# Two feed-forward layers behind an attention: weight loads on another queue, six weight decodes joined by adding transfers, one output block moved to seven products, and a plan with a seed

## The chip, the cores and the metric

The kernel runs on 1 core of a Trainium2 chip. The metric is the device time of one execution in microseconds, the median of three runs. A profiled execution gives the trace that is read here.

## What is computed

A decayed causal attention (4 batches, 8 heads, 576 positions, 64 wide) gives 2304 tokens of 512 features. Two feed-forward layers follow, each with weights of its own, and everything is wanted in float32:

```python
def _moe_ref(x, w_in, w_out):        # layer 0: 512 -> 2048 -> 512
    h = x @ w_in
    g = h - np.tanh(h)
    return g @ w_out

def _moe2_ref(x, w_in, w_out):       # layer 1
    h = x @ w_in
    g = h * (1.0 / (1.0 + np.exp(-h)))
    return g @ w_out
```

The weights reach the chip as raw 64-bit words, which the kernel turns into float32 itself.

## The kernel before

**Products.** Each matrix operand is split in a high part (rounded to the type that TensorE multiplies fast) and a low part (the rest), and a product is three matmuls: high by high, high by low, low by high. A 2 x 2 block product is formed by seven block products with sums of blocks around them instead of eight. ScalarE makes the high parts, VectorE the low parts.

**Work.** A unit is one layer, one set of 512 hidden features (4 sets a layer) and one block of 768 tokens (3 a set): 24 units, 12 for each layer. The first three run beside the end of the attention and in slots of their own; units 3 to 23 are laid out by `joint` (L803). For each unit, `h_step` (L646) runs seven products with the first matrix, 12 matmuls each; then the hidden blocks are gated, added to one another and split (L925 to L989); `c_step` (L713) runs the products with the second matrix, in layer 1 of 18 matmuls of 256 columns each, one unit behind, so that on TensorE a step of unit u's first matrix and one of unit u-1's second alternate. Split inputs go through rings of three tiles: `gr` for hidden blocks, `xr` for inputs, loaded by `ring_load` (L619) on SP's queue. In units 12 to 14, the first set of layer 1, the inputs are not loaded but made from x (`make`, L889) and stored for later sets (`spill`, L634).

**The plain unit.** PLAIN (L40) names unit 13: its second-matrix products are eight plain pieces (`plain_c`, L750; four of 24 matmuls and four of 12, 144 in all), which need only four split hidden blocks, no sums of them, and whose results are copied out by ScalarE (L1072). Set 4, to which it belongs, is in MIXED: its second-matrix weights get a third group (L848).

**Weight decode.** A weight pair (q, m) is two of the sixteen chunks of a layer for matrix m (0 or 1); q runs from 0 to 15, a set has two of them, so set 4 is q = 8, 9 and set 5 is q = 10, 11. `decode` (L830) lists its stages: raw words arrive (two transfers of half a pair, `wload` L156), ScalarE scales the high words (L203), VectorE shifts (L207), takes the exponent (L211), forms the low word's value (L214), joins both by an addition (L226), forms four sums of blocks (L230), then ScalarE casts (L247) and VectorE subtracts (L249) in groups. Temporaries are `wa`, `wb` and `ws`, one of each. As soon as the low word's value is formed, `fill` (L309) issues the next pair's load on SP's queue.

**The order.** `joint` collects tasks with an engine, a cost in steps (a step is 2080 ns), the keys that they read and write, and a wanted time. `planned` (L1125) works from these: each task of an engine other than TensorE gets a latest time by going back from TensorE's order; among those that are ready, the one due first goes next. No task may start more than EARLY = 8 steps before its wanted time. A transfer is a task of the engine "D" with a fixed time; only the first waiting one of "D" is looked at.

Of the kernel before, what the change touches and what calls it, by code (L numbers as in the profile page):

```python
# [1 line left out]

# [12 lines left out]
P = 128  # L15
# [21 lines left out]

U0 = 3
S0 = U0 // 3
PLAIN = (13,)  # L40
PLAINSETS = {s for s in range(NSET, 2 * NSET) if all(NB * s + b in PLAIN for b in range(NB))}
EARLIER = 5
MIXED = {u // NB for u in PLAIN} - PLAINSETS

KA = {1: 1, 2: 2, 3: 4, 4: 0, 5: 6, 6: 3, 7: 5}
# [3 lines left out]
def forgetting_attention_two_ffn(  # L49
# [21 lines left out]
    def rd(ap):  # L71
        return ap.bitcast(F32)
# [80 lines left out]

    raws, wtiles, wjobs = {}, {}, {}

    def wload(q, m, parts=(0, 1)):  # L156
        if q >= 2 * NPR:
            return
        l, c = divmod(2 * q, NFC)
        if (q, m) not in raws:  # L160
            raws[q, m] = rawp.tile([P, 2, DM, 2], U32, tag=f"raw{m}", name=f"raw{q}_{m}")
        for i in parts:
            to = raws[q, m][:, i].rearrange("p n w -> p (n w)")
            nc.sync.dma_start(out=to, in_=(w_in, w_out)[m][l][c + (i if m and q >= 2 * S0 else 1 - i)])

    PLUS, MINUS = ALU.add, ALU.subtract
    RECIPE = (
# [27 lines left out]
    def wjob(q, m, what, part=None):  # L195

        st = wjobs.setdefault((q, m), {})
        l, blocks = 2 * q // NFC, m == 0 or q >= 2 * S0 and q // 2 not in PLAINSETS
        i = slice(0, 2) if part is None else slice(part, part + 1)
        n = f"{q}_{m}"  # L200
        if what == "scale":
            high = rd(raws[q, m][:, i, :, 1])
            nc.scalar.activation(high, high, AF.Prelu, scale=2.0 ** -112, alpha=-(2.0 ** 32))  # L203
        elif what == "shift":
            if "a" not in st:
                st["a"] = wtmp.tile([P, 2, DM], U32, tag="wa", name=f"wa{n}")
            nc.vector.tensor_scalar(st["a"][:, i], raws[q, m][:, i, :, 1], 3, None, ALU.logical_shift_left)  # L207
        elif what == "exponent":
            if "b" not in st:
                st["b"] = wtmp.tile([P, 2, DM], F32, tag="wb", name=f"wb{n}")  # L210
            nc.vector.tensor_scalar(st["b"][:, i].bitcast(U32), st["a"][:, i], 0xFF800000, None, ALU.bitwise_and)  # L211
        elif what == "low":
            b = st["b"][:, i]
            nc.vector.scalar_tensor_tensor(b, raws[q, m][:, i, :, 0], 2.0 ** -52, b, ALU.mult, ALU.mult)  # L214
        elif what == "join":
            if "w" not in st:
                if blocks:
                    st["s"] = wtmp.tile([P, 8, 256], F32, tag="ws", name=f"ws{n}")
                    st["w"] = st["s"][:, 0:4].rearrange(
                        "p (k i) f -> p i k f" if m else "p (i k) f -> p i k f", i=2)  # L220
                else:
                    st["w"] = rd(st["a"])
            a, b = rd(st["a"][:, i]), st["b"][:, i]
            if blocks:
                a, b = (t.rearrange("p i (k f) -> p i k f", k=2) for t in (a, b))
            nc.vector.tensor_tensor(st["w"][:, i], a, b, ALU.add)  # L226
        elif what == "sum":
            s = st["s"]
            to, p, op, r = RECIPE[m * (2 - l)][part]
            nc.vector.tensor_tensor(s[:, to], s[:, p], s[:, r], op)  # L230
        elif what in ("hi", "lo"):
            hi, lo = wtile(q, m)
            frm = st["s"][:, 1:8] if m == 0 else st["w"]
            if m:
                hi, lo = (t.rearrange("p (i k) f -> p i (k f)", i=2) for t in (hi, lo))
            c = i if m else (slice(0, 3), slice(3, 7), slice(7, 8))[part]
            frm = st["s"][:, 0:1] if m == 0 and part == 2 else frm[:, c]
            if what == "hi":
                nc.scalar.copy(hi[:, c], frm)
            else:  # L240
                nc.vector.tensor_tensor(lo[:, c], frm, rd(hi[:, c]), ALU.subtract)
        else:
            for to, n, frm in GROUPS[m and l + 1][part]:
                hi, lo = place(q, to) if m else (w[:, to:] for w in wtile(q, 0))
                hi, lo, frm = hi[:, 0:n], lo[:, 0:n], st["s"][:, frm:frm + n]
# [63 lines left out]
    def fill(j):  # L309
        q, m, *what = j  # L310
        wjob(q, m, *what)
        if what[0] == "low":
            raws.pop((q, m))
            wload(q + 1, m)

    xo, xd, tt = {}, {}, {}

# [485 lines left out]
    def joint():  # L803
# [16 lines left out]
        W2, N2, basis = dve(TB), act(TB), {}  # L820
# [4 lines left out]
        def wkeys(q, m, k):  # L825

            blocks = {0: (0, 1, 2, 3), 3: (1,), 4: (2, 3), 5: (0,)}
            return [("w", q % NSLOT, m, 10 + b) for b in blocks[k]] if m and k in blocks else [("w", q % NSLOT, m, k)]

        def decode(q, m):  # L830

            l = 2 * q // NFC
            job, raw = (lambda *a: lambda: fill((q, m) + a)), ("raw", m)
            yield "D", 3.5, None, (), (raw,), None
            yield "A", act(DM * 2), job("scale"), (raw,), (raw,), None
            yield "V", 0.33, job("shift"), (raw,), ("wa",), None
            yield "V", 0.33, job("exponent"), ("wa",), ("wb",), None
            yield "V", dve(1024), job("low"), (raw,), ("wb", raw), None
# [6 lines left out]
            yield "V", dve(1024), job("join"), ("wa", "wb"), tuple(("ws", k) for k in range(8)), None  # L845
            for k, (to, p, op, r) in enumerate(RECIPE[m * (2 - l)]):
                yield "V", dve(256), job("sum", k), (("ws", p), ("ws", r)), (("ws", to),), None
            groups = [0, 1, 2] if m and q // 2 in MIXED else [0, 1]  # L848
            behind = m and l and q % 2 and 3 * (q // 2) - 1 in PLAIN and q // 2 not in MIXED
            for g in [1, 3, 4, 5] if behind else groups:  # L850
                cols, key = [("ws", k) for to, n, f in GROUPS[m and l + 1][g] for k in range(f, f + n)], wkeys(q, m, g)
                yield "A", act(256 * len(cols)), job("HI", g), cols, key, g
                yield "V", dve(256 * len(cols)), job("LO", g), cols + key, key, None

        def spread(t0, t1, jobs, since):

            total = sum(c for e, c, *_ in jobs if e == "V")
            t = t0
            for e, c, fn, r, w, tag in jobs:
                if e == "D":  # L860
                    task(t - 6, e, c, fn, r, w)
# [27 lines left out]
        def make(u):  # L889
# [13 lines left out]
            for k, i in enumerate(STEPS):  # L903
                n, f = 7 * (u - U0) + k, src[i]
                kr, when = ("xr", n % 3), t0 + 2 * k - 4.6

                def low(n=n, f=f):
                    t = ring_tile(n)
                    tt_(t[:, 1], q[f](), rd(t[:, 0]), MINUS)
                    spill(n)  # L910

                task(when, "A", N2, lambda n=n, f=f: copy(ring_tile(n)[:, 0], q[f]()), (key[f],), (kr,))
                task(when + 0.1, "V", W2, low, (key[f], kr), (kr,))


        for u in range(U0, len(units) + 1):
# [207 lines left out]

    def planned(tasks):  # L1125

        LAG, EARLY = 0.1, 8

        def lag(n, d):

# [504 lines left out]
```

## Time and profile before

| | us |
|---|---|
| median of three runs (899.52 to 899.75) | 899.64 |
| profiled execution | 900.03 |
| its span, first to last instruction | 898.2 |
| TensorE busy | 889.7 |
| VectorE busy | 784.7 |
| ScalarE busy | 602.6 |
| GpSimd busy | 162.8 |

PE is TensorE, PEld its weight loads, DVE VectorE, ACT ScalarE, POOL GpSimd; SPq is the queue of transfers that SyncE issues. Lines are those of the kernel before.

### The profile page before, as it was taken

The numbers are of one execution on the slowest core, as the hardware profiler recorded it, in microseconds if no ns is written. First come the engines' busy times: TensorE is split into PE (matmuls) and PEld (weight loads), VectorE is DVE, ScalarE is ACT, GpSimd is POOL, SyncE is SP. The second block draws the span as 40 slices with busy tenths as digits, with TensorE's granted clock in tenths as the row PEclk, the third lists the DMA queues.
The fourth block names the chain that finished last, engine by engine and source line by source line (L and its number), as shares of the span: only waits on it lengthen the run. The fifth ranks groups of instructions, "written<-read, shape, count | busy, mean of one in ns | idle before, by whom it ended". The sixth has DMA issues, their size and how long they took to land.

```text
span 898.2 us, 16276 instructions
## 1 busy us (share of the span) xinstructions
PE 889.7 (99%) x6079; PEld 845.6 (94%) x6079; DVE 784.7 (87%) x1320; ACT 602.6 (67%) x1008; POOL 162.8 (18%) x242
## 2 busy tenths in 40 slices
PE   8999999999999999999999999999999999999997
PEld 6777777799999999999999999999999999999997
DVE  7799989798889999998999999997997799776647
ACT  6788888765556666766766778866765665555543
POOL 8999999500000000000000000000000000000000
PEclk9999999999999999999999999999999999999999
DMA  5424533477458686787678564787667566555753
GB/s 176 148 97 149 178 122 96 179 280 287 194 224 299 226 279 236 251 305 258 235 269 293 210 249 186 276 281 273 232 243 267 194 223 240 193 178 183 231 170 120
DMA packets 51103, 196.04 MB, mean 218 GB/s; under 512 B 9744, under 2 KB 15120, under 8 KB 50992
## 3 DMA queue, kind: packets, MB, share of 16 engines
q1 hardware_dynamic: 50744, 194.72, 61.4%
q8 instruction: 48, 0.79, 0.3%
q10 hardware_dynamic: 280, 0.28, 0.1%
q14 instruction: 31, 0.25, 0.1%
HBM read 151.98 MB, written 41.88 MB: 216 GB/s over the span
## 4 chain that ended last, share of the span: by engine, by line
PE 94%; POOL 2%; DVE 1%; DMA 1%; ACT 1%; issue 1%; SPq 0%; DVEq 0%; POOLq 0%; ACTq 0%
PE h L656 34%; PE a L732 32%; PE a L431 6%; PE t L1364 5%; PE s L1317 4%; PE out_t L1423 4%; PE h L475 4%; PE a L764 2%; PE s L1309 2%; PE h L461 2%; POOL kqs L1259 1%; POOL p L1352 1%; DMA raw<-w_in 0%; PE out_t L1451 0%; PE out L1423 0%
## 5 line engine op out<-in xcount | busy, mean ns | idle before, releaser
L656 PE MATMUL h<-xr,wh 128*128 128x384 f32 x1176 | 299.1, 335 | 0.0
L656 PEld LDWEIGHTS h<-xr,wh 128*128 128x128 f32 x1176 | 208.7, 188 | 0.4 <-ACT h L944 0.4
L656 PE MATMUL h<-xr,wl 128*128 128x384 f32 x588 | 196.6, 334 | 0.0
L656 PEld LDWEIGHTS h<-xr,wl 128*128 128x128 f32 x588 | 110.4, 188 | 0.0
L987 ACT CAST gr<-f 128x768 fp32r<-128x768 f32 x104 | 86.7, 838 | 32.5 <-PE a L732 29.9
L988 DVE TENSOR_TENSOR gr<-f,gr 128x768 fp32r<-128x768 f32 x104 | 98.6, 950 | 3.9 <-ACT gr L987 3.9
L732 PE MATMUL a<-wh,gr 128*128 128x256 f32 x516 | 99.2, 282 | 0.0
L732 PEld LDWEIGHTS a<-wh,gr 128*128 128x128 f32 x516 | 82.9, 190 | 0.0
L1338 ACT ACTIVATE p<-p,mn 128x128 f32<-128x128 f32 (+3 forms) x128 | 71.3, 559 | 16.4 <-DVE mn L1330 13.8
L1031 DVE TENSOR_TENSOR x<-a,x 128x768 f32<-128x768 f32 x61 | 58.1, 953 | 21.3 <-PE a L732 20.6
L1352 POOL TENSOR_SCALAR p<-p,sm 128x128 f32<-128x128 f32 (+3 forms) x128 | 73.3, 590 | 8.0 <-DVE sm L1349 5.3
L732 PE MATMUL a<-gr,wh 128*128 128x384 f32 x288 | 73.3, 334 | 0.4 <-DVE gr L988 0.4
L732 PE MATMUL a<-weh,gr 128*128 128x256 f32 x380 | 73.3, 282 | 0.0
L732 PE MATMUL a<-wl,gr 128*128 128x256 f32 x258 | 72.8, 282 | 0.0
L1330 DVE CUSTOM_DVE_ANT_0 p<-s,mask 128x128 f32<-128x128 f32 (+3 forms) x128 | 59.5, 478 | 14.1 <-PE s L1317 11.8
L1024 ACT COPY a<-a 128x768 f32<-128x768 f32 x49 | 38.4, 784 | 49.4 <-PE a L732 46.8
L732 PEld LDWEIGHTS a<-weh,gr 128*128 128x128 f32 x380 | 61.1, 190 | 0.2
L944 ACT COPY h<-h 128x768 f32<-128x768 f32 x42 | 33.0, 785 | 35.0 <-PE h L656 33.8
L732 PE MATMUL a<-gr,weh 128*128 128x384 f32 x216 | 54.8, 334 | 0.0
L1259 POOL TENSOR_TENSOR kqs<-kqraw,kqs 128x288 fp32r<-128x288 f32 (+1 forms) x62 | 53.8, 889 | 1.3
L732 PE MATMUL a<-wel,gr 128*128 128x256 f32 x190 | 53.6, 282 | 0.0
L732 PEld LDWEIGHTS a<-gr,wh 128*128 128x128 f32 x288 | 52.0, 188 | 0.8 <-DVE gr L988 0.8
(173 smaller groups left out, 2075.1 us busy)
## 6 DMA issues: line engine op xcount, KB each, us to landing
xr<-xd SPq DMA_DIRECT2D x126, 768.0 KB
raw<-w_in SPq DMA_DIRECT2D x32, 512.0 KB
raw<-w_out SPq DMA_DIRECT2D x32, 512.0 KB
xd<-xo SPq DMA_DIRECT2D x21, 768.0 KB
xd<-xr SPq DMA_DIRECT2D x21, 768.0 KB
kqraw<-kq SPq DMA_DIRECT2D x16, 608.0 KB
aside<-aside SPq DMA_DIRECT2D x15, 384.0 KB
vraw<-v SPq DMA_DIRECT2D x16, 320.0 KB
```

The lines of the kernel that those rows point to most:

```text
L431: nc.tensor.matmul(dst, w, m, start=first and r == 0, stop=last and r == 2)
L656: nc.tensor.matmul(dst[:, j, 0:TH], w[:, ds], m[:, d], start=i in (1, 5) and d == r == 0, stop=d == 1 and r == 2, skip_group_check=True,)
L732: nc.tensor.matmul(dst, w, m, start=fresh and (l == 0 or d != 1) and j == r == 0, stop=j == 1 and r == 2, skip_group_check=True,)
L987: task(w, "A", N2, lambda g=g, f=frm: copy(g[:, 0], f), (kf,), (("gh", kg),))
L988: task(w + 0.1, "V", W2, lambda g=g, f=frm: tt_(g[:, 1], f, rd(g[:, 0]), MINUS), (kf, ("gh", kg)), (("gl", kg),))
L1024: task(when, "A", N2, lambda to=zs, frm=ys: copy(to, frm), (ky,), (kz,), True)
L1031: task(when, "V", W2, lambda: tt_(to, *((frm, to) if op == PLUS else (to, frm)), op), (kf, kx[c]), (kx[c],), True)
L1259: eng.tensor_tensor(lo[:, c0:c1], raw[p][:, c0:c1], rd(hi[:, c0:c1]), ALU.subtract)
L1330: nc.vector.tensor_tensor_reduce(out=pt.rearrange("p (g c) -> p g c", g=2) if i == 4 else pt, in0=src, in1=m, op0=ALU.add, op1=ALU.min, sc ...
L1338: nc.scalar.activation(pt, pt, AF.Exp, bias=mn, scale=-1.0, accum_out=sums[:, n // 3 % 5, n % 3, 0:1],)
L1352: nc.gpsimd.tensor_scalar(pt, pt, sm[:, j:j + 1], 1.0, ALU.mult, ALU.mult)
L1364: nc.tensor.transpose(t[:, k], pt[:, c * P:c * P + P], ident)
```

## The change

- PLAIN is empty. Unit 13's second-matrix products are seven, as in the units around it, set 4 has no third weight group, and no unit has the extra step in `base`.
- ADDED lists 25 of the pairs that `joint` decodes. For these the join adds in place in the temporary that holds the shifted word; every second pair has its blocks 0 to 3 in `wa` and 4 to 7 in `ws`, the others all in `ws`. Groups that cross from block 3 to block 4 of a split pair are cast and subtracted in two pieces. The temporaries are allocated once.
- The load that follows a pair in ADDED is issued from GpSimd's queue, as a task of its own in the plan. Second-matrix rows land in the blocks' order, in two runs for each partition and transfer.
- For six pairs (BYDMA: (8,0), (9,0), (9,1), (10,0), (10,1), (11,0)) the low word's value is written back into the raw tile, and a transfer from GpSimd's queue adds it to the high word instead of VectorE's addition.
- In the plan a load takes 5.5 steps (before 3.5), an adding transfer 4.0, a spill 3.5 (before none); transfers need no longer be taken in the order of their wanted times; EARLY is 12; each latest time is moved by up to 0.2 step by a random number from a fixed seed.

```diff
-PLAIN = (13,)
+PLAIN = ()
+SEED, SPREAD = 5, 0.2
...
+    ADDED = [(2 * S0 + 1, 1)]
+    for g in range(S0, 2 * NSET - 1):
+        o = 2 * g + 1
+        ADDED += [(o, 1), (o + 1, 0), (o + 1, 1), (o + 2, 0)] if g >= NSET else [(o + 1, 0), (o, 1), (o + 1, 1), (o + 2, 0)]
+    ADDED = list(dict.fromkeys(ADDED + [(2 * NPR - 1, 1)]))
+
+    BYDMA = {(NPR, 0), (NPR + 1, 0), (NPR + 1, 1), (NPR + 2, 0), (NPR + 2, 1), (NPR + 3, 0)}
...
+    def block(q, m, k, n=1):
+
+        if (q, m) not in ADDED:
+            return wjobs[q, m]["s"][:, k:k + n]
+        if k + n <= 4 and ADDED.index((q, m)) % 2 == 0:
+            return tmp("wa", [P, 4, 256])[:, k:k + n]
+        return tmp("ws", [P, 8, 256])[:, k:k + n]
...
-    def wload(q, m, parts=(0, 1)):
+    def wload(q, m, parts=(0, 1), queue=None):
...
+            if m and (q, m) in ADDED:
+
+                to = raws[q, m].rearrange("p i n w -> p (i n w)").rearrange("p (k i z) -> p k i z", k=2, i=2)[:, :, i]
+                frm = frm.rearrange("p (k z) -> p k z", k=2)
+            (queue or nc.sync).dma_start(out=to, in_=frm)
...
+            low = rd(row(raws[q, m][:, 0])) if (q, m) in BYDMA else factor
...
+            elif what == "low":
+                nc.vector.scalar_tensor_tensor(low, words[:, :, 0], 2.0 ** -52, factor, ALU.mult, ALU.mult)
+            elif (q, m) in BYDMA:
+                nc.gpsimd.dma_start(out=high, in_=low, accum_op=ALU.add, max_dma_last_dim=8 * DM)
+            else:
+                nc.vector.tensor_tensor(high, high, low, ALU.add)
...
-        if what[0] == "low":
+        if what[0] == ("join" if (q, m) in BYDMA else "low"):
             raws.pop((q, m))
-            wload(q + 1, m)
+            if (q, m) not in ADDED:
+                wload(q + 1, m)
...
-            yield "D", 3.5, None, (), (raw,), None
+            yield "D", LOADING, (lambda: wload(q, m, queue=nc.gpsimd)) if (q - 1, m) in ADDED else None, (), (raw,), "load"
...
+            if added:
+                yield *(("D", ADDING) if (q, m) in BYDMA else ("V", dve(1024))), job("join"), [kept] + wa, wa, None
...
+                task(when + 0.2, "D", SPILLING, None, (kr,), ())
...
-        LAG, EARLY = 0.1, 8
+        LAG, EARLY = 0.1, 12
...
+        shake = random.Random(SEED)
+        latest = [t + SPREAD * shake.uniform(-1, 1) for t in latest]
...
-                known = [(max(r, free[e]), n) for n in waiting[:1 if e in "PSD" else 60] if (r := ready(n)) is not None]
+                known = [(max(r, free[e]), n) for n in waiting[:1 if e in "PS" else 60] if (r := ready(n)) is not None]
```

## Rows read from the trace of the kernel before

**Rows 1.** The page, part 1: busy us, share of the span, instructions.

```profile
PE 889.7 (99%) x6079; PEld 845.6 (94%) x6079; DVE 784.7 (87%) x1320; ACT 602.6 (67%) x1008; POOL 162.8 (18%) x242
```

**Rows 2.** Waits of TensorE: total us, times, longest.

```profile
PE a L732 <- DVE gr L988: 0.4, 1, 0.4
```

**Rows 3.** Windows of the units in `joint`: busy time of each engine.

```profile
core 0: us, PE busy (x) PEld busy (x) DVE busy (x) ACT busy (x) POOL busy (x), PEclk, DMA share, GB/s
300.00:520.00 220.00, 220.00 (x1271) 220.00 (x1270) 209.39 (x269) 149.21 (x195) 0.00 (x0) 1.00 0.76 260
520.00:640.00 120.00, 119.57 (x811) 119.16 (x810) 109.72 (x140) 90.42 (x117) 0.00 (x0) 1.00 0.69 250
...
620.00:640.00 20.00, 20.00 (x144) 20.00 (x143) 12.86 (x16) 13.83 (x18) 0.00 (x0) 1.00 0.80 280
```

**Rows 4.** The chain that ended last: start us, us, what.

```profile
37.20 4.21 DMA raw<-w_in
...
581.31 2.87 PE a L764 x24
...
606.71 4.31 PE a L764 x36
613.10 2.15 PE a L732 x18
```

**Rows 5.** VectorE groups after 262 us: busy us, mean ns of one, idle before.

```profile
L230 DVE TENSOR_TENSOR ws<-ws 128x256 f32<-128x256 f32 x104 | 40.2, 418 | 0.4
...
L226 DVE TENSOR_TENSOR ws<-wa,wb 128x1024 f32<-128x1024 f32 x26 | 31.7, 1220 | 0.4
L249 DVE TENSOR_TENSOR wl<-ws,wh 128x1024 fp32r<-128x1024 f32 x26 | 31.6, 1217 | 1.1 <-ACT wh L247 1.1
...
L988 DVE TENSOR_TENSOR gr<-f_a,gr 128x768 fp32r<-128x768 f32 x20 | 19.0, 952 | 22.8 <-ACT gr L987 22.8
L947 DVE TENSOR_TENSOR f_a<-f,f 128x768 f32<-128x768 f32 x20 | 19.0, 951 | 0.3
...
L249 DVE TENSOR_TENSOR wl<-ws,wh 128x512 fp32r<-128x512 f32 x12 | 8.2, 683 | 0.0
```

**Rows 6.** ScalarE groups after 262 us.

```profile
L987 ACT CAST gr<-f_a 128x768 fp32r<-128x768 f32 x20 | 16.8, 838 | 0.0
```

**Rows 7.** Timeline: a low word on VectorE, then TensorE's product that reads it.

```profile
562.84 0.95 DVE L988 TENSOR_TENSOR gr<-f,gr 128x768 fp32r<-128x768 f32 x1
...
564.22 0.28 PE L732 MATMUL a<-wh,gr 128*128 128x256 f32 x1
```

**Rows 8.** Timeline: decode of (10,0), then of (11,0), to unit 15's first product.

```profile
482.31 0.81 SPq L164 DMA_DIRECT2D raw<-w_in  x2
...
576.53 1.21 DVE L214 SCALAR_TENSOR_TENSOR wb<-raw,wb 128x1024 f32<-128x1024 uint32 x1
577.77 1.50 SPq L164 DMA_DIRECT2D raw<-w_in  x2
...
587.80 1.15 ACT L203 ACTIVATE raw<-raw 128x1024 f32<-128x1024 f32 x1
...
607.45 1.04 ACT L247 CAST wh<-ws 128x1024 fp32r<-128x1024 f32 x1
...
609.86 1.22 DVE L249 TENSOR_TENSOR wl<-ws,wh 128x1024 fp32r<-128x1024 f32 x1
...
610.86 0.52 PE L656 MATMUL h<-xr,wh 128*128 128x384 f32 x2
```

**Rows 9.** Waits of SP's queue after 262 us.

```profile
SPq L164 <- DVE wb L214: 28.6, 18, 6.2
...
SPq L625 <- DMA xd<-xr: 11.1, 2, 7.4
```

**Rows 10.** Line L207 before 180 us, then after: ns min/median/max.

```profile
L207 DVE TENSOR_SCALAR wa<-raw x7: 415/724/1159, 40.2 to 174.5; 128x512 uint32<-128x512 uint32 x6, 128x1024 uint32<-128x1024 uint32 x1
...
L207 DVE TENSOR_SCALAR wa<-raw x28: 678/685/696, 195.5 to 770.5; 128x1024 uint32<-128x1024 uint32 x28
```

**Rows 11.** The page, part 6: issues of transfers.

```profile
raw<-w_in SPq DMA_DIRECT2D x32, 512.0 KB
```

More of the change, by code (lines that the diff above doesn't have):

```diff
@@ L1 @@
+import random
 from contextlib import ExitStack
@@ L154, in forgetting_attention_two_ffn, with tmp, row @@
     raws, wtiles, wjobs = {}, {}, {}
-    def wload(q, m, parts=(0, 1)):
+    ADDED = [(2 * S0 + 1, 1)]
[4 more added lines that the diff above has]
+    BYDMA = {(NPR, 0), (NPR + 1, 0), (NPR + 1, 1), (NPR + 2, 0), (NPR + 2, 1), (NPR + 3, 0)}
+    lasting = {}
+    def tmp(tag, shape, dtype=F32):
+        if tag not in lasting:
+            lasting[tag] = wtmp.tile(shape, dtype, tag=tag, name=f"{tag}_")
+        return lasting[tag]
+    def block(q, m, k, n=1):
[4 more added lines that the diff above has]
+        return tmp("ws", [P, 8, 256])[:, k:k + n]
+    def row(t):
+        return t.rearrange("p k f -> p (k f)")
+    def wload(q, m, parts=(0, 1), queue=None):
         if q >= 2 * NPR:
@@ L162, in wload @@
         for i in parts:
-            to = raws[q, m][:, i].rearrange("p n w -> p (n w)")
-            nc.sync.dma_start(out=to, in_=(w_in, w_out)[m][l][c + (i if m and q >= 2 * S0 else 1 - i)])
+            to, frm = row(raws[q, m][:, i]), (w_in, w_out)[m][l][c + (i if m and q >= 2 * S0 else 1 - i)]
+            if m and (q, m) in ADDED:
+                to = raws[q, m].rearrange("p i n w -> p (i n w)").rearrange("p (k i z) -> p k i z", k=2, i=2)[:, :, i]
+                frm = frm.rearrange("p (k z) -> p k z", k=2)
+            (queue or nc.sync).dma_start(out=to, in_=frm)
     PLUS, MINUS = ALU.add, ALU.subtract
@@ L203, in wjob @@
             nc.scalar.activation(high, high, AF.Prelu, scale=2.0 ** -112, alpha=-(2.0 ** 32))
+        elif (q, m) in ADDED and what in ("shift", "exponent", "low", "join"):
+            high, factor = row(block(q, m, 0, 4)), row(tmp("wb", [P, 4, 256]))
+            if (q, m) in raws:
+                words = raws[q, m].rearrange("p i n w -> p (i n) w")
+            low = rd(row(raws[q, m][:, 0])) if (q, m) in BYDMA else factor
+            if what == "shift":
+                nc.vector.tensor_scalar(high.bitcast(U32), words[:, :, 1], 3, None, ALU.logical_shift_left)
+            elif what == "exponent":
+                nc.vector.tensor_scalar(factor.bitcast(U32), high.bitcast(U32), 0xFF800000, None, ALU.bitwise_and)
+            elif what == "low":
[4 more added lines that the diff above has]
+                nc.vector.tensor_tensor(high, high, low, ALU.add)
         elif what == "shift":
@@ L227, in wjob @@
         elif what == "sum":
-            s = st["s"]
             to, p, op, r = RECIPE[m * (2 - l)][part]
-            nc.vector.tensor_tensor(s[:, to], s[:, p], s[:, r], op)
+            to, p, r = (block(q, m, k) for k in (to, p, r))
+            nc.vector.tensor_tensor(to, p, r, op)
         elif what in ("hi", "lo"):
@@ L242, in wjob @@
         else:
-            for to, n, frm in GROUPS[m and l + 1][part]:
+            pieces = [(to, n, frm) for to, n, frm in GROUPS[m and l + 1][part]]
+            if (q, m) in ADDED and ADDED.index((q, m)) % 2 == 0:
+                pieces = [
+                    piece for to, n, frm in pieces
+                    for piece in ([(to, 4 - frm, frm), (to + 4 - frm, n - 4 + frm, 4)] if frm < 4 < frm + n else [(to, n, frm)])
+                ]
+            for to, n, frm in pieces:
                 hi, lo = place(q, to) if m else (w[:, to:] for w in wtile(q, 0))
-                hi, lo, frm = hi[:, 0:n], lo[:, 0:n], st["s"][:, frm:frm + n]
+                hi, lo, frm = hi[:, 0:n], lo[:, 0:n], block(q, m, frm, n)
                 if what == "HI":
@@ L818, in act @@
             return (n / 0.96 + 60) / 2080
-        W2, N2, basis = dve(TB), act(TB), {}
+        W2, N2, basis, LOADING, ADDING, SPILLING = dve(TB), act(TB), {}, 5.5, 4.0, 3.5
         base = {U0: 0}
@@ L833, in decode @@
             job, raw = (lambda *a: lambda: fill((q, m) + a)), ("raw", m)
-            yield "D", 3.5, None, (), (raw,), None
+            yield "D", LOADING, (lambda: wload(q, m, queue=nc.gpsimd)) if (q - 1, m) in ADDED else None, (), (raw,), "load"
             yield "A", act(DM * 2), job("scale"), (raw,), (raw,), None
-            yield "V", 0.33, job("shift"), (raw,), ("wa",), None
-            yield "V", 0.33, job("exponent"), ("wa",), ("wb",), None
-            yield "V", dve(1024), job("low"), (raw,), ("wb", raw), None
+            added = (q, m) in ADDED
+            own = added and ADDED.index((q, m)) % 2 == 0
+            blk = [("wa" if own and k < 4 else "ws", k) for k in range(8)]
+            wa = blk[0:4] if added else [("wa", k) for k in range(4)]
+            if added and ADDED.index((q, m)) == 0:
+                wa = wa + [("ws", k) for k in range(8)]
+            yield "V", 0.33, job("shift"), (raw,), wa, None
+            wa = wa[0:4]
+            yield "V", 0.33, job("exponent"), wa, ("wb",), None
+            kept = (raw if (q, m) in BYDMA else "wb")
+            yield "V", dve(1024), job("low"), (raw, "wb"), ("wb", raw), None
             if m and q // 2 in PLAINSETS:
@@ L844, in decode @@
                 return
-            yield "V", dve(1024), job("join"), ("wa", "wb"), tuple(("ws", k) for k in range(8)), None
+            if added:
+                yield *(("D", ADDING) if (q, m) in BYDMA else ("V", dve(1024))), job("join"), [kept] + wa, wa, None
+            else:
+                yield "V", dve(1024), job("join"), ["wb"] + wa, tuple(("ws", k) for k in range(8)), None
             for k, (to, p, op, r) in enumerate(RECIPE[m * (2 - l)]):
-                yield "V", dve(256), job("sum", k), (("ws", p), ("ws", r)), (("ws", to),), None
+                yield "V", dve(256), job("sum", k), (blk[p], blk[r]), (blk[to],), None
             groups = [0, 1, 2] if m and q // 2 in MIXED else [0, 1]
@@ L850, in decode @@
             for g in [1, 3, 4, 5] if behind else groups:
-                cols, key = [("ws", k) for to, n, f in GROUPS[m and l + 1][g] for k in range(f, f + n)], wkeys(q, m, g)
+                cols, key = [blk[k] for to, n, f in GROUPS[m and l + 1][g] for k in range(f, f + n)], wkeys(q, m, g)
                 yield "A", act(256 * len(cols)), job("HI", g), cols, key, g
@@ L860, in spread @@
                 if e == "D":
-                    task(t - 6, e, c, fn, r, w)
+                    task(t - 6 * (tag == "load"), e, c, fn, r, w)
                     continue
```

## The prediction

> **What bounds the kernel now.** I read five views in this order. The page's busy shares come first: TensorE is busy 889.7 of 898.2 us, VectorE 784.7, ScalarE 602.6, GpSimd 162.8 [rows 1]. The reader should see that nothing can be gained but by giving TensorE less to do, and that VectorE is the next to bind. The waits of TensorE confirm it: in the whole stretch that the change touches (from about 262 us) it waits once, 0.43 us, for a VectorE low word [rows 2, 3]. The windows then say how near VectorE is to the edge: between 300 and 520 us it is busy 209.39 of 220 us, between 520 and 640 us 109.72 of 120, and of the 10.28 us idle there 7.14 lie after 620 us; the granted clock is 1.00 (the 2.4 GHz level) all along and GpSimd does nothing [rows 3]. The timeline shows what 95% means for a single product: a low word ends at 563.79 us and the product that reads it starts at 564.22, 0.43 us later [rows 7]. So TensorE sets the end, and VectorE keeps up with a few tenths of a microsecond in hand.
>
> The sum is made against the profiled execution: 900.03 us, of which 898.2 are the span and 1.83 lie around it. The median of three runs, 899.64, is 0.39 below it, and I take that off at the end.
>
> **TensorE.** With PLAIN empty, unit 13 (second layer, first set, second block of tokens) forms its output by seven products instead of eight plain pieces. In the chain a plain piece of 24 matmuls takes 2.87 us and three pieces of 12 together 4.31, a product of 18 takes 2.15 [rows 4]. Four pieces of each kind are 4 x 2.87 + 4 x 1.44 = 17.24 us; seven products 7 x 2.15 = 15.05. Difference: **-2.2 us**; by matmuls, 144 - 126 = 18 at 2.15/18 us, it is 2.15, which I use. The 0.43 us wait may stay or go; I leave it in and keep its removal for the low end.
>
> **VectorE.** Unit 13 now needs what its neighbours need: three sums of gated blocks, one more for the fourth, and three more low words of ring tiles, 7 x 0.95 = +6.66 us (the rows with f_a stand for all of them) [rows 5]. The change of basis at L1086 moves: unit 16 loses it, unit 13 gains one subtraction of the same width, nothing in sum. Set 4 loses its separate third group, two 256-wide low words, -0.84. Six joins go to transfers, 6 x 1.22 = -7.31. In 13 of the 25 decodes (every second one in ADDED) a low-word group is cut at the boundary between two temporaries: 2 x 0.683 - 1.217 = 0.15 us each, +1.9 in all [rows 5]. Sum: **+0.4 us**. By place: four of the six joins ((9,1), (10,0), (10,1), (11,0)) lie in 520 to 640 us, so that window gets 6.66 - 4.87 + 0.45 for three cuts, less up to 0.84, which is 1.4 to 2.2 us, and has 2.15 us less time, against 10.28 us idle [rows 3, 5]. The second decode of set 5, due only at unit 16, can move behind 620 us. It is therefore costed at nothing: the cover is that idle time, and if the order doesn't reach it, TensorE waits for the rest, up to 4 us.
>
> **ScalarE** gets three more casts at 0.84 us, three seeds and four copies in place of the four copies of plain pieces, and 13 cuts: below 10 x 0.84 = 8.4 us near unit 13, where it is busy 90.42 of 120 us [rows 3, 6]. Nothing on the path.
>
> **Queues.** 23 weight loads (46 transfers of 512 KB [rows 11]) leave SP's queue for GpSimd's. On SP they waited 28.6 us in 18 waits for a decode, and the loads of ring tiles stood behind them [rows 9]; TensorE never waited for a ring tile [rows 2], so that gain is zero now. On GpSimd's queue a waiting load holds up only other loads and the six accumulating transfers; the engine itself is idle there [rows 3]. The plan books 5.5 steps (11.4 us, a step being 2.08 us in the code) for a load. One 512 KB half took 4.21 us where the chain shows it [rows 4], so two are at most 8.4: within the booking, cost nothing. Splitting second-matrix rows in two halves doubles their packets; bound 0 to 4.2 us on a landing, inside the remaining 3 us or just over it; I take 0, as the nearest row leaves room.
>
> **The accumulating transfer** has no row. A lower bound is the 4.21 us of a plain 512 KB load, an upper one the longest wait for a stored ring tile, 7.4 us [rows 4, 9], and since such a transfer must also read its destination it could take twice that, 14.8. The plan books 4 steps, 8.3 us. I take about 6, nearest to the two measured rows. The Trainium skill, "DMA: Bandwidth & Descriptors", section "Anatomy of one DMA — SWDGE (gpsimd) path", gives 2.0 us plus bytes over 436 GB/s; an estimate by that page is 3.2 us for 512 KB, and the sum would be the same. No row here shows it.
>
> What is late next if it is slow: the decode of (11,0), needed at unit 15's first product. In the trace its scaling starts at 587.80 us, its high words at 607.45, its low words end at 611.08, and that product's first half starts at 610.86, with (11,0) read in the second half, a microsecond later [rows 8]. The work between scaling and high words is 1.15 + 2 x 0.69 + 1.22 + 1.22 + 4 x 0.42 = 6.65 us [rows 5, 8, 10] of 19.65, so 13.0 us are spare. Two accumulating transfers lie in that line, (10,0)'s, behind which (11,0)'s load now waits, and its own; each takes the place of a 1.22 us join, and the deadline is 2.15 us earlier. At 6 us each they eat 2 x 4.8 + 2.15 = 11.7 of the 13.0. Fits.
>
> **Order.** EARLY from 8 to 12 steps, transfers that no longer queue behind one another in the plan, the second temporary and the spills as stages give the plan more to choose from. The seed moves each deadline by up to 0.2 step, 0.42 us, as much as the 0.43 us margin [rows 7]: bounds 0.43 gained and, if one product in a unit is late by that, some 10 units x 0.2 = 2 lost; I take 0, since the only loss in the trace is a single wait [rows 2].
>
> **Sum:** 900.03 - 2.15 - 0.39 = **897.5 us**, 0.24% below the median. About 0.2% (1.8 us) is what a measurement of this kernel can tell from no change, so the forecast stands only just beyond it.
>
> **Rivals.**
> *Thin margin.* A VectorE order that puts a 1.22 us decode step ahead of a low word makes TensorE wait 0.8 us (1.22 less 0.43) [rows 5, 7]. Against it: one such wait in 600 us. For it: VectorE has 6.66 us more to do around unit 13 and shifted deadlines. Two such waits give 897.5 + 1.6 = 899.1: within 0.2%.
> *The accumulating transfers are late.* Place: (11,0) before unit 15. If (10,0) is not decoded earlier than now, TensorE waits once each transfer exceeds (13.0 - 2.15)/2 + 1.22 = 6.6 us, and the change turns slower by over 0.2% once the wait exceeds 2.15 + 1.8 us, at 8.6 us each. At 10 us: 2 x 8.8 + 2.15 - 13.0 = 6.7 us, **904.2 us**; at the upper bound of 14.8 some 914. For it: the DMA engines are busy 0.69 of this window [rows 3]. Against it: the plan books 8.3 us, and (10,0)'s data lie ready long before its low words are made at 576.53 us, since its load went out at 482.31 [rows 8].
> *GpSimd and VectorE hold each other up.* While GpSimd computes, early in the kernel, the 1024-wide shift takes up to 1.159 us; afterwards, with GpSimd idle, never more than 0.696 [rows 10]. Writing descriptors may bring that back: 0.47 us for each of the two such operations in a decode, some 8 in the stretch without idle time, up to 3.8 us: 901.3 if all are met, 899 if some. The Trainium skill, "SBUF — State Buffer", section "SBUF: two separate sides", warns against this very move: a transfer issued from GpSimd has its descriptors delayed while VectorE runs an operation of two ports. By that rule loads start at most 0.7 us later, within the booking, so the trace prices the other direction higher.
> *Nothing is gained*, the seven products simply running as long as eight pieces, is excluded by rows 4.
>
> **Chances.** Forecast 0.53; thin margin 0.18; mutual blocking 0.06; late transfers 0.23. Faster 0.53, same 0.24 (the second and third), slower 0.23. The range starts at 896.9, 0.43 us for the wait and some scatter below the forecast, and goes to 902.5, which takes in the two cases in the middle and the mildest of the late transfers; about 2 in 10 stay outside.
>
> **What would show it.** TensorE's lines lose the 24- and 12-matmul pieces, seven products of 2.15 us stand between some 581 and 609 us, interleaved with unit 14's first-matrix products; 600 to 640 us carries 2 us less; TensorE's waits for VectorE, ScalarE or a transfer after 262 us total under 0.8 us; the add of wa and wb appears six times less; shifts keep 0.69 us. I am wrong if TensorE waits at unit 15's first product, if a join's transfer takes over 8.6 us, or if shifts stretch towards 1.1 us.

## The result and the profile after

The changed kernel takes 905.06 us (median of 6 runs, 904.31 to 905.75) against 899.6 for the kernel before (6 runs beside it, 899.52 to 899.75): a ratio of 1.0059, 95% interval 1.0048 to 1.0069. It is slower, by 5.5 us, where 2.1 us less was forecast. The profiled execution took 904.72 us with a span of 902.8, 4.6 more than before.

The page, part 1, of the kernel after (columns as in [rows 1]):

```profile
PE 889.8 (99%) x6061; PEld 845.0 (94%) x6061; DVE 784.2 (87%) x1332; ACT 607.0 (67%) x1025; POOL 197.4 (22%) x294
```

TensorE runs 18 matmuls fewer and yet is as long busy as before, 889.8 to 889.7 us [rows 1]. VectorE is down by 0.5 us. What TensorE waits for from 262 us on stands in the view of waits (total, times, longest), in place of the single 0.4 us of [rows 2]:

```profile
PE h L713 <- DMA xr<-xd: 3.6, 2, 3.4
...
PE h L713 <- ACT h L1013: 1.3, 1, 1.3
```

And the windows, the first three those of [rows 3], the last three cut out of the second:

```profile
300.00:520.00 220.00, 220.00 (x1271) 220.00 (x1270) 207.96 (x272) 149.10 (x200) 16.56 (x25) 1.00 0.77 265
520.00:640.00 120.00, 114.99 (x755) 113.34 (x754) 108.63 (x141) 91.53 (x121) 8.67 (x13) 0.99 0.73 260
...
620.00:640.00 20.00, 20.00 (x135) 20.00 (x135) 13.27 (x18) 13.22 (x17) 2.57 (x4) 0.94 0.81 296
...
610.00:615.00 5.00, 4.70 (x32) 4.32 (x31) 4.96 (x8) 3.76 (x6) 0.00 (x0) 1.00 1.02 420
615.00:620.00 5.00, 1.66 (x7) 1.69 (x8) 4.93 (x8) 2.56 (x3) 0.00 (x0) 0.91 0.92 334
620.00:625.00 5.00, 5.00 (x29) 5.00 (x29) 1.28 (x2) 2.07 (x3) 1.45 (x2) 0.75 0.85 310
```

TensorE's waits lie between 582 and 619 us, in the steps of unit 14's first matrix and the first of unit 15's. Behind the 3.4 us wait the granted clock falls: 0.75 over five microseconds, so partly at the lower level, 1.2 GHz. The chain of waits gives the order of events (start, us, what):

```profile
571.30 9.52 DMA x<-aside
...
580.84 0.97 DVE f_tmp L965
...
583.49 0.70 ACT h L1013
...
601.24 12.23 DMA xd<-xr
...
613.53 4.67 DMA xr<-xd
...
618.34 3.57 PE h L713 x12
621.90 2.46 PE a L789 x18
624.37 2.08 PE h L713 x12
626.45 2.15 PE a L789 x18
```

The first two products after the wait take 3.57 and 2.46 us, the next two 2.08 and 2.15: 1.8 us are the clock's. The span adds up: 898.2 - 2.15 (matmuls) - 0.43 (the old wait) + 4.9 (the two lines of waits) + 2.25 (889.8 less 889.7 - 2.15: busier, 1.8 of it by the clock) = 902.8.

Two collisions of transfers are in that chain. The timeline of GpSimd's and SyncE's queues and of VectorE in the kernel after (start, us, engine and line; in brackets what ended the idle time before). Where no view prints a landing, the text gives the last update of the transfer's semaphore in the trace:

```profile
564.91 0.91 POOL L251 DMA_DIRECT2D ws__3958<-raw  x1 [50.08 <-ACT f L1013]
570.14 1.09 POOL L198 DMA_DIRECT2D raw<-w_in  x2 [4.31 <-DMA ws__3958<-raw]
...
571.30 1.10 SPq L733 DMA_DIRECT2D x<-aside  x1
...
580.84 0.96 DVE L965 TENSOR_TENSOR f_tmp<-x 128x768 f32<-128x768 f32 x1 [3.32 <-DMA x<-aside]
...
598.49 0.95 DVE L977 TENSOR_TENSOR xr<-x,xr 128x768 fp32r<-128x768 f32 x1
...
600.83 0.32 SPq L682 DMA_DIRECT2D xr<-xd  x1
601.24 2.16 SPq L695 DMA_DIRECT2D xd<-xr  x2
...
602.10 0.95 DVE L977 TENSOR_TENSOR xr<-x,xr 128x768 fp32r<-128x768 f32 x1
...
605.07 1.11 POOL L198 DMA_DIRECT2D raw<-w_in  x2 [5.85 <-DMA ws__3958<-raw]
...
613.53 25.97 SPq L682 DMA_DIRECT2D xr<-xd  x8
```

The same places in the kernel before:

```profile
572.68 1.00 SPq L676 DMA_DIRECT2D x<-aside  x1
...
578.93 0.95 DVE L897 TENSOR_TENSOR f_tmp<-x 128x768 f32<-128x768 f32 x1
...
592.21 0.95 DVE L909 TENSOR_TENSOR xr<-x,xr 128x768 fp32r<-128x768 f32 x1
593.18 0.33 SPq L638 DMA_DIRECT2D xd<-xr  x1
...
603.23 0.33 SPq L625 DMA_DIRECT2D xr<-xd  x1
```

```profile
610.00:615.00 5.00, 5.00 (x39) 5.00 (x38) 5.00 (x7) 3.08 (x5) 0.00 (x0) 1.00 0.58 198
```

*First collision.* At 564.91 GpSimd's queue issues the adding transfer of (10,0). Once it has landed, at 570.14, the queue sends the load of (11,0), 1 MB. 1.16 us later SyncE's queue sends the load of a set-aside block of x that unit 14's inputs need. That load lands after 9.5 us and VectorE stands still for 3.32 us. Before, it was issued at 572.68 and VectorE started on it at 578.93 without a wait, and it took 5.7 us; (11,0) came only after it, at 577.77 [rows 8]. TensorE's wait of 1.3 us follows through ScalarE: it casts the late tile at 581.83, and only behind that, at 583.49, does it copy the earlier result that TensorE waits for.

*Second collision.* Unit 14's last input tile is made at 602.10 (before: 600.48). The store of the tile before it leaves at 601.24, between an adding transfer (597.12) and 1 MB of (11,1) (597.72) on one side and, at 605.07, 1 MB of (12,0) on the other. The store lands after 12.2 us, and only then, at 613.53, may SyncE's queue load unit 15's second tile into the ring place that the store was read from. It lands at 618.20, and TensorE has had nothing to do for 3.4 us. The store is not only slow, it also starts late. Its tile's low word is made at 598.49 (before: 592.21), and the store stands behind the ring load of 600.83, so it leaves 8.1 us later than before (593.18). Before, it landed after 5.8 us, and the ring load (603.23) did not have to wait for it. Of the 14.5 us by which the store lands later, 8.1 are its start and 6.4 its way. Between 610 and 615 us the transfer engines are full, share 1.02, 420 GB/s; before they stood at 0.58 there.

The transfers that the forecast worried about were on time. The page, part 6, of the kernel after (issue, count, size, median us to landing):

```profile
raw<-w_out POOLq DMA_DIRECT2D x24, 512.0 KB, 6.8
raw<-w_in POOLq DMA_DIRECT2D x22, 512.0 KB, 7.2
...
wa__3938<-raw POOLq DMA_DIRECT2D x3, 512.0 KB, 6.8
ws__3958<-raw POOLq DMA_DIRECT2D x3, 512.0 KB, 5.5
```

### The profile page after: what moved, and what is told of

The parts are those of the page before. It is cut to its first block, busy times and chain, and to the rows that moved or that the text cites. A ratio compares the mean times of both kernels' runs of the same rounds, so it can differ in the third digit from the quotient of the medians.

```text
span 902.8 us, 16319 instructions
## 1 busy us (share of the span) xinstructions
PE 889.8 (99%) x6061; PEld 845.0 (94%) x6061; DVE 784.2 (87%) x1332; ACT 607.0 (67%) x1025; POOL 197.4 (22%) x294
## 4 chain that ended last, share of the span: by engine, by line
PE 92%; DMA 3%; DVE 2%; ACT 1%; issue 1%; DVEq 0%; SPq 0%; ACTq 0%
PE h L713 32%; PE a L789 32%; PE t L1437 5%; PE s L1390 5%; PE a L488 5%; PE out_t L1496 5%; PE h L532 4%; PE s L1382 2%; PE h L518 1%; DMA xd<-xr 1%; DMA x<-aside 1%; DMA xr<-xd 1%; PE out L1496 0%; PE out_t L1524 0%; DVE gr L1057 0%
## 5 line engine op out<-in xcount | busy, mean ns | idle before, releaser
L789 PE MATMUL a<-wh,gr 128*128 128x256 f32 x564 | 108.8, 283 | 0.0
L789 PEld LDWEIGHTS a<-wh,gr 128*128 128x128 f32 x564 | 91.0, 191 | 0.0
L789 PE MATMUL a<-weh,gr 128*128 128x256 f32 x416 | 80.1, 282 | 0.0
L789 PE MATMUL a<-wl,gr 128*128 128x256 f32 x282 | 79.7, 283 | 0.0
L198 POOL DMA_DIRECT2D raw<-w_out x24 | 17.7, 751 | 242.2 <-DVE ws__3958 L245 98.1
L1093 ACT COPY a<-a 128x768 f32<-128x768 f32 x52 | 40.8, 785 | 42.6 <-PE a L789 42.5
L789 PEld LDWEIGHTS a<-weh,gr 128*128 128x128 f32 x416 | 66.9, 190 | 0.0
L789 PE MATMUL a<-wel,gr 128*128 128x256 f32 x208 | 58.7, 282 | 0.0
```

What stands on the lines that cost most here:

```text
L789: nc.tensor.matmul(dst, w, m, start=fresh and (l == 0 or d != 1) and j == r == 0, stop=j == 1 and r == 2, skip_group_check=True,)
```

## The experiments

The theory after reading both traces: weight loads freed from their queue run beside the transfers that unit 14's inputs need, and VectorE, with seven products' sums to form, has no time left to absorb it. The rivals: the adding transfers, the seven products by themselves, the seed, and a plan that doesn't know of the store before a ring load. "Before" was run beside every version; its median was 899.58 to 899.83 us, with single runs up to 902.4.

**The parts apart.** Four versions each undo one part of the change, or make one part alone.

```diff
--- after
+++ e1_plain13
-PLAIN = ()
+PLAIN = (13,)
--- after
+++ e2_sp_loads
-(lambda: wload(q, m, queue=nc.gpsimd)) if (q - 1, m) in ADDED else None
+(lambda: wload(q, m, queue=nc.sync)) if (q - 1, m) in ADDED else None
--- after
+++ e3_no_adding
-    BYDMA = {(NPR, 0), (NPR + 1, 0), (NPR + 1, 1), (NPR + 2, 0), (NPR + 2, 1), (NPR + 3, 0)}
+    BYDMA = set()
--- before
+++ e4_only_seven
-PLAIN = (13,)
+PLAIN = ()
```

> The changed kernel with unit 13 plain again (eight pieces), all else of the change kept. Theory A (weight loads that start the moment an adding transfer lands take the transfer engines from the load of the set-aside block and from the stored input tiles of unit 14): the two waits of TensorE, 1.3 and 3.4 us, stay, so the time is 899.6 + 2 to 7 us, 902 to 907. Rival B (seven products give VectorE 6.7 us more to do, so unit 14's tiles are made late): no such waits, 899.6 within 0.7 us, and the set-aside block still lands in under 7 us.

> The changed kernel, its plan untouched, with the weight loads issued from SP's queue instead of GpSimd's. If it is GpSimd's queue as such (a second queue that shares the engines), the waits of TensorE at about 584 and 615 us go: 898 to 900. Theory A in its form 'when the loads start, whatever the queue': the load of the set-aside block still stands behind 1 MB, so the wait at 584 us stays at 0.5 to 2 us; SP's queue also stands still while a load waits for an adding transfer, so 903 to 908. Rival B expects 904 to 906, unchanged.

> The changed kernel without adding transfers: all 25 joins are VectorE additions again. Theory A: loads now start when the low word's value is made, no longer at the landing, and 3 MB less move around 565 to 610 us; the waits for transfers shrink to under 1.5 us, 898 to 901. Rival B: VectorE has 7.3 us more to do, unit 14's tiles are later still, 906 or more. Rival C (the adding transfers themselves are late for unit 15's weights): the waits go altogether, 897.5 to 898.5.

> The kernel before with one edit, unit 13 by seven products. Rival B: unit 14's tiles or weights are late here too, TensorE waits 3 us or more, 900 to 905. Theory A: the transfers go out as before (set-aside block ahead of the weight load), so TensorE never waits for a transfer there; 897.5 to 899.5, any wait being for VectorE.

| version | us (lowest to highest, runs) | ratio to before, interval |
|---|---|---|
| e1, eight pieces again | 899.32 (898.88 to 902.66, 10) | 0.9996, 0.9986 to 1.0006 |
| e2, loads on SyncE's queue | 901.46 (898.59 to 902.59, 10) | 1.0010, 0.9999 to 1.0021 |
| e3, no adding transfers | 902.14 (900.69 to 903.65, 8) | 1.0023, 1.0012 to 1.0033 |
| e4, seven products alone | 900.42 (900.01 to 901.78, 10) | 1.0003, 0.9994 to 1.0012 |

The time of e1 lies in the range of the rival that blames the seven products, against the theory; e4 lies in that rival's range too, but with a shorter wait than the rival asked for; e2 and e3 lie in no range that was expected. TensorE's waits after 262 us in e1:

```profile
PE h L713 <- DMA xr<-xd: 0.3, 1, 0.3
```

In e2:

```profile
PE h L713 <- DMA xr<-xd: 3.5, 2, 1.9
```

In e3:

```profile
PE h L713 <- DVE xr L977: 2.8, 1, 2.8
PE a L789 <- DVE gr L1057: 0.3, 1, 0.3
```

In e4:

```profile
PE a L732 <- DVE gr L988: 2.0, 1, 2.0
```

Neither half of the change costs anything alone: all of it but the seven products gives 899.3 (e1), the seven products alone 900.4 (e4). Together they give 905.1, some 5 us more than the two add up to. That is an interaction, and e2 and e3 say of what. With the loads on SyncE's queue, 3.6 us of the loss are gone; (11,0) stands there behind the set-aside load again (576.16 after 575.05), and VectorE waits for that 0.47 us instead of 3.32. In e1 the loads leave as early as in the kernel after ((11,0) at 570.19) and the transfer engines are as full (0.95 in 570 to 580 us, 0.98 in 600 to 610), and yet nothing waits but once for 0.3 us: the set-aside load leaves 3.8 us behind (11,0) there instead of 1.2 and takes 6.0 us, and VectorE's tiles for unit 14 are done by 597.2 instead of 603.1. The adding transfers have a part in the loss: without them 2.9 us of it are gone (905.06 to 902.14). The store that took 12.2 us takes 7.0 in e3, though there VectorE has the joins to do, its busy time is 789.7 instead of 784.2 us, and TensorE waits for VectorE itself. Whether it is the 3 MB that no longer move, or the other times at which loads leave, e3 doesn't tell. e4 shows a wait for VectorE by itself: in the windows of 600 to 620 us of e4 VectorE has no idle time left, and the clock is 0.91 behind the wait:

```profile
600.00:620.00 20.00, 18.02 (x116) 17.62 (x115) 19.97 (x27) 14.15 (x20) 0.00 (x0) 0.91 0.72 248
```

So the 2.15 us that seven products save are taken back by a VectorE wait of 2.0 us and the clock.

**The plan.** Two versions change what `planned` knows or draws.

```diff
--- after
+++ e8_ring_planned
+            for k in range(3 if b == NB - 1 else 0):
+                task(t0 + 8.1 + 2 * k, "D", 2.5, None, (), (("xr", (7 * (u + 1 - U0) + k) % 3),))
--- after
+++ e11_no_seed
-SEED, SPREAD = 5, 0.2
+SEED, SPREAD = 5, 0.0
```

> The changed kernel with three more timed stages in the plan: the loads of unit 15's first three ring tiles, which must wait for unit 14's last three stores (2.5 steps each). Nothing else is edited; the order follows from the plan. Theory D: VectorE makes unit 14's tiles several us earlier, no wait for a ring tile over 0.8 us: 897.5 to 900. Theory A: the stores still meet the weight loads, waits of 2 us or more: 901 to 904.

> The changed kernel with SPREAD = 0: deadlines are not moved. If the seed's order makes the waits (theory E), they go: 897.5 to 899.5. Theories A and B: the same two places wait, 902 to 907.

e8: 905.37 us (904.65 to 906.97, 4 runs), ratio 1.0064, 1.0049 to 1.0079; unit 14's tiles are made at the same times as in the kernel after, and TensorE waits 2.8 and 1.8 us at the same two places. e11: 906.22 us (904.54 to 907.49, 4 runs), ratio 1.0064, 1.0047 to 1.0081; its waits are 4.8 (longest 4.5) and 0.7 us. Neither edit removes the loss. The stage by itself doesn't help: with it the plan still counts 7.3 us for a store (3.5 steps) that takes 12.1. That doesn't clear the plan of the lateness of unit 14's tiles, and its other edits (EARLY, the longer loads, the free order of transfers) were not undone one by one. Without the seed the kernel is no faster.

**Holding a load by a GpSimd read.** To keep the loads on GpSimd's queue but behind the transfers that they disturb, GpSimd reads one column of the awaited tile first: e5 holds (11,0) behind the set-aside block, e6 holds (12,0) behind unit 15's second ring tile, e7 both.

```diff
--- after
+++ e7_hold_both
+            n = fns.index(marks[mark]) + 1
+            fns[n:n] = [lambda: nc.gpsimd.tensor_scalar(seen, what(), 1.0, 1.0, ALU.mult, ALU.mult)] + moved
...
+        hold([(11, 0)], ("aside", 14), lambda: xblock(2, 0, 0)[:, 0, 0:1])
+        hold([(12, 0)], ("h", 14, 5), lambda: rd(ring_tile(85))[:, 0, 0, 0:1])
```

> The changed kernel, same plan, but GpSimd reads one number of the set-aside block of unit 14 before it issues the load of (11,0), so that this load no longer runs beside that block's. Theory A (collision of transfers): the block lands in under 6.5 us instead of 9.5, VectorE's 3.3 us of idle time before it and TensorE's wait of 1.3 us go, and with 3.3 us given back to VectorE the later wait of 3.4 us falls below 2: 900 to 902.5. Theory D (unit 14's input tiles are made just in time because the plan knows nothing of the way store, then load, of the same ring place): only the 1.3 us and the clock behind it go, the wait for the ring tile at unit 15 stays at 3 us or more: 902.5 to 904.5.

> The changed kernel, same plan, but the load of (12,0), which started at 605 us between the last stores of unit 14, is held until unit 15's second input tile has landed. Theory A: the two last stores land in 6 to 8 us instead of 10 to 12, the ring tile's wait falls from 3.4 to under 1.5 us: 901 to 903. Theory D: the store is issued too late anyway (601 us), the wait stays at 2.5 us or more: 903.5 to 905.5.

> Both holds together. Theory A: no wait of TensorE over 0.8 us after 262 us: 897.5 to 899.5, faster than the kernel before. Theory D: the ring tile's wait at unit 15 is still there with 1.5 us or more: 900 to 903.

| version | us (lowest to highest, runs) | ratio to before, interval |
|---|---|---|
| e5 | 907.47 (900.20 to 908.69, 10) | 1.0071, 1.0049 to 1.0093 |
| e6 | 903.50 (902.37 to 905.46, 5) | 1.0041, 1.0026 to 1.0056 |
| e7 | 906.88 (899.01 to 908.55, 10) | 1.0062, 1.0037 to 1.0086 |

e5 and e7 fall in two heaps: two of ten runs at 900.2 and 901.4 (e5) or 899.0 and 899.7 (e7), the others at 906.6 and above. The timeline of GpSimd in e5, whose profiled run was one of the two:

```profile
577.45 0.18 POOL L1202 TENSOR_SCALAR seen<-x 128x1 f32<-128x1 f32 x1 [11.25 <-DMA x<-aside]
578.05 1.14 POOL L198 DMA_DIRECT2D raw<-w_in  x2 [0.42 <-issue]
...
593.77 0.90 POOL L251 DMA_DIRECT2D ws__3959<-raw  x1 [7.93 <-ACT gr L1058]
```

The same in e7, whose profiled run was one of the eight:

```profile
576.98 12.37 POOL L1202 TENSOR_SCALAR seen<-x 128x1 f32<-128x1 f32 x1 [11.27 <-DMA x<-aside]
...
600.84 0.89 POOL L251 DMA_DIRECT2D ws__3959<-raw  x1 [9.46 <-ACT a L1095]
...
620.61 0.18 POOL L1202 TENSOR_SCALAR seen<-xr 128x1 f32<-128x1 f32 x1 [17.67 <-DMA xr<-xd]
```

Neither e5 nor e7 lies in a range that was expected. In e7's profiled run the hold cost more than what it was to remove: the first such read took 12.37 us in e7 and 0.18 in e5, (11,0) was decoded 7 us later for it, and TensorE waited 7.9 us once. Only the profile of e7 shows this; that e5's eight longer runs have the same cause is likely from their times, not shown. What e5's profile does show is the first collision undone: the set-aside block lands after 5.7 us instead of 9.5, VectorE doesn't wait, and of TensorE's waits only the second is left (2.4 us). In e6 the store still takes 10.8 us, and with (12,0) behind it ScalarE stands still for the weights, 3.64 us, and TensorE for ScalarE, 2.1 us: a hold that late has a price of its own.

**Moving transfers in the order of SyncE's queue.** No engine reads anything for it. e9 moves the set-aside load ahead of unit 13's fourth store; e10 adds the load of (12,0) on SyncE's queue behind unit 15's second ring tile. In both, unit 14's first input tile is formed from the set-aside block in place of x's own; operations and sizes are the same.

```diff
--- after
+++ e9_aside_early
+        move(marks["aside", 14], ("x", 13, 3), 0)
--- e9_aside_early
+++ e10_both_moved
+        move(loading[12, 0], ("h", 14, 5), 1)
```

> The changed kernel, same plan, but the load of the set-aside block of unit 14 is moved up in SP's queue, ahead of four stores (some 13 us), so that it can't meet the load of (11,0). Theory A: it lands long before VectorE wants it; VectorE's 3.3 us of idle time and the wait at 584 us go; unit 14's tiles are made 3 us earlier; the ring tile's wait at unit 15 stays at 2 to 3 us, since 5 MB still want to move between 594 and 610 us: 900 to 902. If VectorE's amount of work alone decides (theory B), the idle time moves to another place and the time stays at 903 to 905.

> As the run before, and the load of (12,0), which started at 605 us between unit 14's last stores, goes out on SP's queue behind unit 15's second ring tile. Theory A: the last stores land in under 9 us, no wait of TensorE over 1 us at unit 15, and none after it as (12,0) is scaled at 627 us: 897.5 to 899.5. Theory B: 901 or more, with a wait for VectorE.

e9: 900.61 us (899.08 to 901.85, 10 runs), ratio 1.0005, 0.9996 to 1.0015; VectorE no longer waits for the block, and one TensorE wait of 2.8 us is left, at the second collision (the view of waits names a scaling on ScalarE that ends 0.05 us after the ring load's landing; the product reads the ring tile and not what was scaled). e10: 898.55 us (897.67 to 900.08, 10 runs), ratio 0.9987, 0.9978 to 0.9996; two waits together 0.8 us. Each collision has its own price: 4.5 us (905.06 to 900.61) for the first with what followed from it, 2.1 for the second.

**Versions that compute all of it.** The same without moving the set-aside load: (11,0) goes on SyncE's queue right behind it (e13), (12,0) too behind unit 15's second ring tile (e12); the other 21 loads stay on GpSimd's queue. e14 also issues unit 15's first ring load after the second-last store instead of ahead of it.

```diff
--- after
+++ e13_one_behind
+        move(loading[11, 0], ("aside", 14), 1)
--- e13_one_behind
+++ e12_two_behind
+        move(loading[12, 0], ("h", 14, 5), 1)
--- e12_two_behind
+++ e14_store_first
-        ring_load(7 * (u - U0) + k + 3)
+        if (u, k) != (14, 4):
+            ring_load(7 * (u - U0) + k + 3)
+        fns.insert(fns.index(marks["x", 14, 5]) + 1, lambda: ring_load(84))
```

> As the run before with (11,0) alone moved; (12,0) stays on GpSimd's queue and starts between the last stores. Theory A: the first wait (1.3 us) goes, the ring tile's wait at unit 15 stays at 2 to 3 us: 899.5 to 902. If (11,0)'s collision was the whole of it: 897.5 to 898.5, as the run before.

> The changed kernel, same plan and all parts of the change, but two of its 23 weight loads go out on SP's queue: (11,0) right behind the set-aside block of unit 14, (12,0) right behind unit 15's second ring tile. Theory A: the set-aside block lands in under 7 us, the last stores in under 11, TensorE waits less than 1.5 us in all after 262 us: 897.5 to 899.5, at or below the kernel before. Theory B (the amount of VectorE's work): 901 or more, with a wait for VectorE.

> The run with two loads behind, and one more move on SP's queue: the load of unit 15's first ring tile is issued behind the store of unit 14's second-last input tile instead of ahead of it. Theory A: that store is issued 1.5 to 2 us earlier and with no 768 KB ahead of it, lands by 606 us instead of 608.3, and the wait for the ring tile (1.9 us) falls below 0.5: 897.3 to 898.3, faster than the kernel before by about the 2.15 us of unit 13. If the 5 MB between 594 and 612 us are what bounds it, whatever their order, another transfer is late instead: 899 to 900.

| version | us (lowest to highest, runs) | ratio to before, interval |
|---|---|---|
| e13 | 900.74 (899.16 to 901.81, 12) | 1.0003, 0.9994 to 1.0012 |
| e12 | 899.39 (897.85 to 901.93, 11) | 0.9996, 0.9987 to 1.0004 |
| e14 | 898.59 (897.85 to 900.59, 11) | 0.9990, 0.9981 to 0.9999 |

TensorE's waits after 262 us in e12:

```profile
PE h L713 <- DMA xr<-xd: 1.9, 1, 1.9
```

The timeline of SyncE's queue in e12: both loads of weights behind what they must not disturb, and a store (597.53) that a ring load (608.30) waits for:

```profile
570.98 1.02 SPq L733 DMA_DIRECT2D x<-aside  x1
572.22 1.74 SPq L198 DMA_DIRECT2D raw<-w_in  x2
...
597.53 2.05 SPq L695 DMA_DIRECT2D xd<-xr  x2
608.30 0.32 SPq L682 DMA_DIRECT2D xr<-xd  x1
```

TensorE's waits in e14:

```profile
PE h L713 <- DVE gr L1061: 1.5, 1, 1.5
```

And SyncE's queue in e14, the loads of unit 15's first ring tile and of its second:

```profile
597.05 0.32 SPq L682 DMA_DIRECT2D xr<-xd  x1
...
605.76 0.32 SPq L682 DMA_DIRECT2D xr<-xd  x1
```

The product that waits, on TensorE in e14:

```profile
609.10 0.59 PE L713 MATMUL h<-xr,wh 128*128 128x384 f32 x2 [1.46 <-DVE gr L1061]
```

One load of the 23, sent 1.24 us behind the set-aside load instead of 1.16 us ahead of it, is worth 4.3 us (905.06 to 900.74). In e13 unit 14's second-last tile is made at 595.06 instead of 598.49, so the first collision made the store late too; a wait of 2.5 us for the ring tile is left, with the clock at 1.00. The second load moved (e12) brings 1.3 more and the store's place (e14) 0.8, differences within the scatter of the runs. e14 is the one version here that computes all of it and is faster than both kernels, by 0.1%, its interval only just below 1. In it the load of the second ring tile leaves 2.5 us earlier than in e12, and what is late next is another transfer. The view of waits names VectorE's low word of a hidden block, whose semaphore moves at 608.98, but the product reads no hidden block. It reads unit 15's first ring tile, and that tile's load, sent at 597.05 behind the store now, landed at 608.96, after 11.9 us (e12: at 606.36, after 9.3). So the time lies between the two ranges expected, and the late transfer is the one that the second of them spoke of.

## Why the prediction was wrong, point by point

- **TensorE, -2.15 us: right.** Where the clock stayed at 1.00, busy time is 887.2 (e9) and 887.3 (e14), against 889.7 - 2.15 = 887.55.
- **VectorE, +0.4 in sum: right in size** (784.2 after, 784.7 before). **Its cover was wrong.** "It is therefore costed at nothing: the cover is that idle time": of 10.28 us idle, 7.14 lay after 620 us, and the need was before 610. In the kernel after, unit 14's second-last input tile is made 6.3 us later than before; by e13, 3.4 of these come from the first collision. The bound that the prediction kept, "up to 4 us", is what e4 shows, a 2.0 us wait and the clock behind it.
- **Queues, nothing: the step that failed.** The prediction asked whether the moved loads would land in time and whether TensorE had waited for the queue that they left. It didn't ask what they would take from the transfers that stayed, and e13 puts a number on that: 4.3 us for one load. "TensorE never waited for a ring tile, so that gain is zero" was true, but the old order protected something. Before, (11,0) left at 577.77, behind the set-aside load, once (10,0)'s low word was formed [rows 8]; the new plan decodes (10,0) earlier, and a load on a queue of its own goes as soon as its raw tile is free, at 570.14, ahead of that load. The row that spoke of this, "SPq L625 <- DMA xd<-xr" with its 7.4 us [rows 9], was used as a price for the adding transfers and not as what it is, a store that a ring load waits for; in the kernel after, such a store took 12.2 us. The bound on a load was too low as well: "two are at most 8.4" rests on one half early in the kernel, while here the halves took up to 11.7 us and the pair of (11,1) 12.4, over the booking of 11.4; TensorE waited for none of them. The Trainium skill, "DMA: Bandwidth & Descriptors", sections "Issuing engines are not separate DMA queues" and "Queues, rings and completion order", says that transfers of all issuing engines run on the same 16 engines, which take turns between queues. The traces agree on the sharing: the set-aside load took 9.5 us with the other queue's load ahead of it, and 5.7 us when that load came after it (e5). No run here shows the turns.
- **Adding transfers, about 6 us: right.** They landed in 4.6 to 7.6 us, median 6.2. So the rival on the other side, with 904.2 us, met the size and the place (unit 15's first products) by luck, not by the mechanism: (11,0) was in time, and unit 15's second input tile was not.
- **The clock was not in the sum.** It added 1.8 us behind the wait of 3.4.
- **GpSimd and VectorE holding each other up: didn't happen.** The shifts of the kernel after take 683 to 696 ns in all 25 decodes of ADDED, as in [rows 10].
- **The seed, nothing: right** (e11). The 0.43 us wait of [rows 2] is gone, as the low end of the range allowed.

What stays open is the rest of the lateness of unit 14's tiles (595.06 in e13, 592.21 before): how much of it is the work of seven products and how much VectorE's order, which around 594 us puts decode steps of 0.69 to 1.22 us ahead of them. Open is also what other times for the adding transfer and the load of (11,1) would bring, beside which the last two stores still take 10 to 13 us in e12 to e14. No version tried either.

## What to carry to other kernels

When transfers move to another queue, list what their old queue kept them behind: a load that leaves earlier is a load that runs beside something else, and its price is on the other's landing. Spare time of an engine covers an edit only if it lies before the point of need, so cut the window there. And two edits that are each free can use up the same reserve: e1 and e4 cost nothing, together they cost 5 us.

## What the runs showed that was not expected

- A one-column operation on GpSimd, the first after a long stretch in which it only issued transfers, took 12.37 us in e7, 0.48 in e6 and 0.18 in e5; the second one in e7 took 0.18.
- The view of waits names what ended last by the profile. In e14 two ends lay 0.02 us apart, and the one named was not what the product reads.
- The clock does not follow from the length of the wait alone: it fell behind waits of 3.4 us (kernel after), 2.8 (e3, 0.83 over 600 to 620 us), 2.0 (e4) and 1.9 (e12, 0.91 over the same stretch), and stayed at 1.00 behind 2.8 (e9) and 2.5 (e13).
- An adding transfer of 512 KB lands as soon as a plain one: median 5.5 and 6.8 us for its two destinations, against 6.8 and 7.2 for plain loads on the same queue.
